# Routed experts behind windowed attention: the first round's chain ahead of the second round's work, the first rows ahead of second-layer weights, and full-height digit matmuls

## The chip, the core and the metric

The kernel runs on one core of a Trainium2 chip. The metric is the device time of one execution in microseconds. Before the change the median of three runs is 535.29 us (534.54 to 538.76). The profiled execution is a fourth one, of 538.62 us; its trace spans 536.9 us, so 1.7 us lie outside the span. TensorE is PE, its weight load PEld, VectorE DVE, ScalarE ACT, GpSimd POOL, and SyncE, which issues most transfers, SP.

## The reference

```python
scores = where(sink or in_window, scale * q @ k.T, -1e9)     # 4 batches, 8 heads, 768 tokens, head_dim 64
x = softmax(scores) @ v                                       # 3072 tokens x 512
logits = x @ w_gate                                           # 8 experts, capacity 384 each
for idx in argsort(-logits.flatten()):                        # greedy: best (token, expert) pair first
    tok, e = idx // E, idx % E
    if assigned[tok] >= 0 or counts[e] >= cap: continue
    assigned[tok] = e; counts[e] += 1
for e in range(E):
    out[assigned == e] = relu(x[assigned == e] @ w1[e]) @ w2[e]   # w1 512x1024, w2 1024x512
```

## The kernel before, in words

**Attention** fills the first 163 us. It writes the tokens to a buffer in HBM and leaves the gate values in `L`.

**Rounds.** The greedy assignment is done in eight rounds (`phase`, k = 0 to 7). Round k finds the one expert that fills up next, and its 384 tokens. It looks for a threshold digit by digit, six digits: DVE compares (`cmp`), 12 or 6 small matmuls count (`cnt`, line 529), DVE turns the counts into eight zeros and ones (`i8`, line 551), one matmul sums them with a constant matrix (`dp`, line 555), DVE takes the maximum (`P`, line 557). Before, `i8` is used to a height of 64 or 32 rows, so that the matmul at line 555 stands on 64 or 32 rows of the array. Then comes the expert's number (`ei`, line 568), a ranking (lines 573 to 598, matmuls at 576, 577 and 602), and the list of tokens (`idx`, lines 606 to 609). Lines 612 to 617 erase the chosen expert and tokens for the next round, and lines 468 to 486 prepare the next round's digits.

**Experts.** Each round feeds one expert. SP reads `ei` and issues eight loads of 512 KB (line 633): chunks 0 to 3 are w1, 4 to 7 are w2. Four buffers `raw` hold them, so chunk 4 may start once chunk 0 has been used. Of each chunk ACT makes a rounded copy `wh` (line 635) and DVE the rest `wl` (line 637). POOL gathers the 384 rows in three indirect transfers `xg` (line 642); PE transposes them (line 650, 12 transposes), and ACT and DVE make `xh` and `xl` (652, 653). The first layer has eight blocks f of four steps, each of three matmuls (line 663); the blocks share two accumulators `ph`, so block f waits until ACT (`hh`, 666) and DVE (`hl`, 667) have emptied block f-2. The second layer has three tiles of eight steps, three matmuls each (675). ACT empties them (678), POOL scatters them (680).

**Order.** Every engine works in order. A list scheduler writes the order of all rounds and experts (`Graph.order`): its priority is the longest remaining path plus a number from the table `BIAS` for the class of the operation (W weights, H hidden, T erasing, and so on, with the round). `warm` (505) puts matmuls without use into PE's gaps until the first expert starts. Rounds and experts overlap: round k+1 is computed while expert k is.

Of the kernel before, what the change touches and what calls it, by code (L numbers as in the profile page):

```python
# [349 lines left out]
CAP=384  # L350
# [62 lines left out]
class Moe:  # L413
# [4 lines left out]
    def __init__(self,ctx,tc,L,idn):  # L418
# [3 lines left out]
        def t(shape,dt,name): return c.tile(shape,dt,name=name)  # L422
# [19 lines left out]
        self.cmp=[t([128,64*NC],BF,f"cmp{j}") for j in range(2)]  # L442
        self.i8=t([128,E+1],BF,"i8"); self.odd=t([64,2*E],F32,"odd"); self.two=t([64,2*E],F32,"two"); self.sw=t([128,3],F32,"sw"); self.P=[t([128,1],F32,f"P{j}") for j in range(2)]
        self.w8=t([128,E],F32,"w8"); self.mx8=t([128,1],F32,"mx8"); self.sel=t([128,E],F32,"sel")
        self.M=t([128,2,NC],BF,"M"); self.xae=t([128,2,NC],F32,"xae"); self.sc=t([128,2*NC],BF,"sc"); self.q=t([128,2,NC],F32,"q"); self.c4=t([128,NC,7],F32,"c4"); self.edge=t([128,6],F32,"edge")
        for j in range(6): g.memset(self.edge[:,j:j+1],64.0*j+63.5)
        self.R=t([128,NC,6],F32,"R"); self.R3=t([128,NC,6],F16,"R3")
        self.ei=[t([1,1],I32,f"ei{j}") for j in range(E)]; self.idx=[t([128,3],I32,f"idx{j}") for j in range(E)]
        self.done=0
    def fill(self,j,n):  # L450
# [56 lines left out]
    def phase(self,g,k):  # L507
        nc=self.nc; V=nc.vector; L=self.L; last=k==E-1; first=k==0; cls=f'R{k}'; slow=2 if first else 1
        u=lambda x: 69+x/.96
        def v(cost,fn,r,w,n=''): return g.add('V',cost,fn,r.split(),w.split(),f'R{k}.{n or w.split()[0]}',cls)  # L510
        def e(cost,fn,r,w,n=''): return g.add('E',cost,fn,r.split(),w.split(),f'R{k}.{n or w.split()[0]}',cls,lat=165)
# [3 lines left out]
        if not last:  # L515
# [6 lines left out]
            for n,(sh,m) in enumerate(STEPS):  # L522
# [27 lines left out]
                v(73,lambda src=src,m=m: V.tensor_scalar(odd[0:m,0:E],src,-1.0,None,op0=OP.mult),tn,'odd')  # L550
                v(73,lambda top=top,m=m: V.scalar_tensor_tensor(self.i8[0:m,0:E],top,float(CAP)-0.5,odd[0:m,0:E],op0=OP.subtract,op1=OP.is_ge),tn+' odd','i8')

                dp,bn=bank()
                wt=self.wt[0] if n==0 else self.wt[1] if n<5 else self.onesb
                e(110,lambda m=m,dp=dp,wt=wt: nc.tensor.matmul(dp[:,0:E],wt[:m],self.i8[:m,0:E],start=True,stop=True),'i8',bn,f'dp{n}')  # L555
                P=self.P[n%2]; Pn=f'P{n%2}'
# [52 lines left out]
        v(75,lambda: V.tensor_tensor(self.idx[k][64:128],r2[64:128,1,:,1],sw[64:128],OP.add),bn+f' swb idxa{k}',f'idx{k}')  # L609
        cls=f'T{k}'  # L610
        if not last:
            v(94,lambda: V.tensor_scalar(self.sel,self.w8,self.mx8,NEG,op0=OP.is_equal,op1=OP.mult),'w8 mx8','sel')
            v(269,lambda: V.tensor_tensor(L,L,self.sel[:,None,:].to_broadcast([128,NC,E]),OP.add),'L sel','L')
            v(138,lambda: V.scalar_tensor_tensor(self.clo,self.w8,self.mx8,self.clo,op0=OP.is_equal,op1=OP.add),'w8 mx8 clo','clo')
            v(u(NC),lambda: V.tensor_tensor(self.m3,c4[:,:,0],c4[:,:,6],OP.subtract),'c40 c4','m3')
# [187 lines left out]
```

## Time and profile before

| | us |
|---|---|
| median of three runs | 535.29 |
| profiled execution | 538.62 |
| its span | 536.9 |
| attention ends, round 0 starts | 163 |
| first matmul of the first expert | 201.85 |
| last matmul of the last expert | 529.8 |

To read it: a timeline row has the start, the duration, the engine, the line, the operation with its output and inputs, and in brackets how long the engine stood idle before and what ended that. Matmuls are pipelined, so their durations overlap; the distance from one start to the next is what a matmul costs. The granted clock is a share of 2.4 GHz; 0.50 is 1.2 GHz.

### The profile page before, as it was taken

The page shows a single profiled execution, that of the slowest core. Times are in us where ns is not written, and L with a number is a line of the kernel's source. Part 1 is how long each engine was busy: PE and PEld are TensorE (multiplying, and loading weights), DVE is VectorE, ACT ScalarE, POOL GpSimd, SP SyncE. Part 2 cuts the span into 40 slices and gives each one's busy share as a digit, 9 for nine tenths or more (in the row PEclk, how much of TensorE's full clock was granted, in tenths as well). Part 3 has the DMA queues.
Part 4 walks back from the last instruction along what each step waited for, and adds up shares of the span by engine and source line. Part 5 has one row for each costly group of instructions (what it writes and reads, how often), then busy time and mean ns, then how long its engine had stood idle before and what let it go on. Part 6 is the DMA issues. An engine that isn't in the chain of part 4 may idle for free.

```text
span 536.9 us, 11136 instructions
## 1 busy us (share of the span) xinstructions
PE 491.7 (92%) x4009; PEld 405.4 (76%) x4009; DVE 351.3 (65%) x1112; ACT 247.8 (46%) x714; POOL 148.6 (28%) x205
## 2 busy tenths in 40 slices
PE   6899999998995589989999999999999999999994
PEld 4687787787883258858877878777788778898983
DVE  2766767767676887965986986887878544541110
ACT  4788887888850043351261451343343334631210
POOL 4667665665440020030040310021310330101001
PEclk7899999999997599998999999999999999999998
DMA  7466665566311280560560641643713644610101
GB/s 238 149 191 175 182 181 169 160 177 169 92 42 40 91 282 2 181 211 2 169 251 13 208 165 59 212 143 108 265 60 123 212 145 153 231 60 20 40 10 50
DMA packets 74935, 72.88 MB, mean 136 GB/s; under 512 B 28032, under 2 KB 57472, under 8 KB 74880
## 3 DMA queue, kind: packets, MB, share of 16 engines
q1 hardware_dynamic: 71040, 59.58, 36.2%
q0 software_dynamic: 3840, 12.59, 6.5%
q8 instruction: 32, 0.52, 0.4%
q14 instruction: 23, 0.19, 0.1%
HBM read 59.57 MB, written 12.58 MB: 134 GB/s over the span
## 4 chain that ended last, share of the span: by engine, by line
PE 60%; DVE 14%; DMA 13%; ACT 7%; issue 3%; SPq 0%; POOLq 0%; POOL 0%; ACTq 0%; DVEq 0%
PE ph L663 19%; PE py L675 15%; DMA raw<-w 10%; PE pp L112 7%; PE pp L74 6%; ACT P L89 4%; DVE wl L637 3%; PE pp L95 3%; PE pp L124 3%; PE pr L529 2%; DMA xg<-x_dram,idx 2%; PE pp L121 2%; ACT wh L635 2%; DVE cmp L459 1%; PE pt L650 1%
## 5 line engine op out<-in xcount | busy, mean ns | idle before, releaser
L635 ACT ACTIVATE wh<-raw 128x1024 fp32r<-128x1024 f32 x64 | 67.6, 1059 | 96.7 <-DMA raw<-w 61.9
L637 DVE TENSOR_TENSOR wl<-raw,wh 128x1024 fp32r<-128x1024 f32 x64 | 78.1, 1221 | 31.4 <-ACT wh L635 30.9
L663 PE MATMUL ph<-xh,wh 128*128 128x384 f32 x256 | 92.7, 362 | 0.0
L663 PE MATMUL ph<-xl,wh 128*128 128x384 f32 x256 | 86.8, 339 | 0.0
L663 PE MATMUL ph<-xh,wl 128*128 128x384 f32 x256 | 86.7, 339 | 0.0
L675 PE MATMUL py<-wh,hh 128*128 128x512 f32 x192 | 78.9, 411 | 1.2 <-ACT yo L678 1.2
L680 POOL DMA_INDIRECT out<-yo,idx x24 | 25.3, 1053 | 196.7 <-ACT yo L678 134.7
L675 PE MATMUL py<-wh,hl 128*128 128x512 f32 x192 | 75.7, 394 | 0.0
L675 PE MATMUL py<-wl,hh 128*128 128x512 f32 x192 | 75.5, 393 | 0.0
L89 ACT ACTIVATE P<-pp,nmx 128x132 f32<-128x132 f32 x192 | 69.1, 369 | 10.1 <-DVE nmx L84 8.4
L666 ACT ACTIVATE hh<-ph 128x384 fp32r<-128x384 f32 x64 | 31.3, 489 | 85.6 <-PE ph L663 68.8
L642 POOL DMA_INDIRECT xg<-x_dram,idx x24 | 28.4, 1182 | 122.9 <-PE pr L555 69.2
L74 PE MATMUL pp<-kk,q 64*128 64x260 f32 (+1 forms) x384 | 58.5, 406 | 2.2 <-ACT P L89 0.8
L667 DVE SCALAR_TENSOR_TENSOR hl<-ph,hh 128x384 fp32r<-128x384 f32 x64 | 35.2, 554 | 38.7 <-ACT hh L666 38.2
L663 PEld LDWEIGHTS ph<-xh,wh 128*128 128x128 f32 x256 | 49.0, 191 | 4.3 <-issue 0.7
L79 DVE COPY_PREDICATED pp<-mprev,pp 128x256 f32<-128x256 int32 x80 | 34.0, 424 | 26.9 <-PE pp L104 16.5
L663 PEld LDWEIGHTS ph<-xl,wh 128*128 128x128 f32 x256 | 48.6, 190 | 2.8 <-DVE xl L653 0.2
L663 PEld LDWEIGHTS ph<-xh,wl 128*128 128x128 f32 x256 | 48.4, 189 | 0.0
L97 POOL TENSOR_SCALAR_AFFINE_SELECT A<-PT 128x512 f32<-128x512 f32 x48 | 31.1, 647 | 49.4 <-ACT PT L96 49.4
L675 PEld LDWEIGHTS py<-wh,hl 128*128 128x128 f32 x192 | 36.0, 188 | 8.7 <-DVE hl L667 0.7
L675 PEld LDWEIGHTS py<-wh,hh 128*128 128x128 f32 x192 | 36.4, 190 | 7.9 <-ACT yo L678 2.0
L84 DVE TENSOR_REDUCE nmx<-pp 128x2 f32<-128x264 f32 x96 | 40.8, 429 | 1.5
(145 smaller groups left out, 843.0 us busy)
## 6 DMA issues: line engine op xcount, KB each, us to landing
raw<-w SPq DMA_DIRECT2D x64, 512.0 KB, 5.0
v<-vd SPq DMA_DIRECT2D x24, 256.0 KB, 3.5
x_dram<-xt SPq DMA_DIRECT2D x24, 256.0 KB, 2.9
kk<-kd SPq DMA_DIRECT2D x23, 264.0 KB, 3.7
q<-qd SPq DMA_DIRECT2D x23, 256.0 KB, 3.8
xg<-x_dram,idx POOLq DMA_INDIRECT x24, 4.9
out<-yo,idx POOLq DMA_INDIRECT x24, 2.8
us<-ud SPq DMA_DIRECT2D x1, 288.0 KB, 4.4
```

What stands on the lines that cost most here:

```text
L74: PE.matmul(sp[:,s,:n],q[p,g,:],kk[p,g,k0:k0+n],start=True,stop=True)
L79: V.copy_predicated(sp[:,:,132:260],mprev[:,None,:].to_broadcast([128,2,128]),sp[:,:,0:128])
L84: V.tensor_reduce(T('nmx',c)[:,2*g:2*g+2],sp[:,:,o:o+132],AX.X,OP.max,negate=True)
L89: A.activation(T('P',c)[:,h,:],sp[:,s,o:o+132],AF.Exp,bias=T('nmx',c)[:,h:h+1],scale=1.0,accum_out=T('sm',c)[:,h:h+1])
L97: def op_A(c,g): G.affine_select(T('A',c)[:,4*g:4*g+4],T('PT',c)[:,4*g:4*g+4],[[0,4],[1,128]],OP.is_ge,0.0,base=0,channel_multiplier=-1)
L112: PE.matmul(av[64*s:64*s+64,hp-2*g,:],T('v',j)[:,h*64:h*64+64],T(x,c)[:,h,:],start=hp==2*g and x=='A',stop=x=='B' or not i,skip_group_chec ...
L635: g.add('A',947,lambda wh=wh,raw=raw: nc.scalar.activation(wh,raw,AF.Copy),[f'raw{n%4}'],[f'wh{s}'],f'H{k}.{j}',f'W{k}')
L637: g.add(e,{'V':1135,'P':2303}[e],lambda wh=wh,wl=wl,raw=raw,e=e: (nc.vector if e=='V' else nc.gpsimd).tensor_tensor(wl,raw,wh.bitcast(F32) ...
L663: nc.tensor.matmul(p[:,0:CAP],x[:,c,:],y[:,c,:],start=c==0 and i==0,stop=c==3 and i==2)
L666: g.add('A',371,lambda f=f,p=p: nc.scalar.activation(self.hh[:,f,:],p[:,0:CAP],AF.Relu),ps,[f'hh{f}'],f'hh{k}.{f}',f'H{k}')
L667: g.add('V',469,lambda f=f,p=p: nc.vector.scalar_tensor_tensor(self.hl[:,f,:],p[:,0:CAP],0.0,self.hh[:,f,:].bitcast(F32),op0=OP.max,op1=OP ...
L675: nc.tensor.matmul(p,x[:,f,ts],w,start=f==0 and i==0,stop=f==7 and i==2)
```

## The change: what it does

Four things. The array `i8` becomes two arrays, zeroed once; the matmul at line 555 uses all 128 rows of one of them. In round 0 the erasing (lines 612, 614, 615) gets a dependency on the token list `idx`. For expert 0 a register load that reads the third gathered tile, and a dependency on it, stand before chunks 4 to 7; nothing uses the register. In the built program the load itself is not there, only its waits: in SP's order the waits for the third gather (and for what was issued before it) stand in the row ahead of the first w2 load of expert 0. The table `BIAS` has other numbers in all entries.

```diff
-        self.i8=t([128,E+1],BF,"i8"); ...
+        self.i8=[t([128,E],BF,f"i8{j}") for j in range(2)]; ...
+        for x in self.i8: g.memset(x,0.0)
...
-                v(73,lambda top=top,m=m: V.scalar_tensor_tensor(self.i8[0:m,0:E],top,float(CAP)-0.5,odd[0:m,0:E],op0=OP.subtract,op1=OP.is_ge),tn+' odd','i8')
+                v(73,lambda top=top,m=m,z=z: V.scalar_tensor_tensor(self.i8[z//4][0:m],top,float(CAP)-0.5,odd[0:m,0:E],op0=OP.subtract,op1=OP.is_ge),tn+' odd',f'i8{z//4}')
...
-                e(110,lambda m=m,dp=dp,wt=wt: nc.tensor.matmul(dp[:,0:E],wt[:m],self.i8[:m,0:E],start=True,stop=True),'i8',bn,f'dp{n}')
+                e(60,lambda z=z,dp=dp,wt=wt: nc.tensor.matmul(dp[:,0:E],wt,self.i8[z//4],start=True,stop=True),f'i8{z//4}',bn,f'dp{n}')
...
-        cls=f'T{k}'
+        cls=f'T{k}'; aft=f' idx{k}' if first else ''
...
-            v(94,lambda: V.tensor_scalar(self.sel,self.w8,self.mx8,NEG,op0=OP.is_equal,op1=OP.mult),'w8 mx8','sel')
+            v(94,lambda: V.tensor_scalar(self.sel,self.w8,self.mx8,NEG,op0=OP.is_equal,op1=OP.mult),'w8 mx8'+aft,'sel')
...
+            if k==0 and j==4:
+
+                g.add('S',100,lambda: nc.sync.value_load(self.xg[2][0:1,0:1].bitcast(I32)),['xg2'],['rowed'],'rowed','L0')
...
-            g.add('D',1460,ld,[f'reg{k}'],[f'raw{n%4}'],f'L{k}.{j}',f'L{k}')
+            g.add('D',1460,ld,[f'reg{k}']+(['rowed'] if k==0 and j>3 else []),[f'raw{n%4}'],f'L{k}.{j}',f'L{k}')
...
-            self.weights(g,k); self.rows(g,k); self.mlp(g,k)
+            if k==0: self.rows(g,k); self.weights(g,k); self.mlp(g,k)
+            else: self.weights(g,k); self.rows(g,k); self.mlp(g,k)
...
-BIAS={'G0': -792535, 'G1': -546488, ...
+BIAS={'G0': 295629, 'G1': 162254, ...
```

The order of the attention part is the same on every engine. Behind it the new table moves work on all of them. Line numbers of the change are one higher than before from line 449 on, and four higher from line 633 on.

**DVE, the end of round 0.** `sw` and `idx` are the token list, `di`, `xb`, `cmp<-xb` are round 1's digits, `wl` is expert 0's first weights. Before:

```order
416 L475 TENSOR_TENSOR s<-vm,f 128x24
417 L477 TENSOR_SCALAR di<-s 128x24
418 L478 TENSOR_SCALAR di<-s 128x24
419 L482 TENSOR_SCALAR di<-s 128x24
420 L606 TENSOR_SCALAR sw<-pr_2411 64x3
421 L607 TENSOR_SCALAR sw<-pr_2411 64x3
422 L479 CAST xb_103<-di 128x24
423 L608 TENSOR_TENSOR idx_142<-pr_2411,sw 64x3
424 L483 TENSOR_SCALAR di<-s 128x24
425 L459 TENSOR_TENSOR cmp_109<-xb_103,grid 128x1536
426 L609 TENSOR_TENSOR idx_142<-pr_2411,sw 64x3
```

With the change:

```order
402 L599 TENSOR_TENSOR R_134<-R,tid 128x144
403 L607 TENSOR_SCALAR sw<-pr_2414 64x3
404 L608 TENSOR_SCALAR sw<-pr_2414 64x3
405 L609 TENSOR_TENSOR idx_143<-pr_2414,sw 64x3
406 L610 TENSOR_TENSOR idx_143<-pr_2414,sw 64x3
407 L613 TENSOR_SCALAR sel<-w_118,mx_119 128x8
408 L616 TENSOR_TENSOR m_98<-c_125 128x24
409 L615 SCALAR_TENSOR_TENSOR clo<-w_118,mx_119,clo 128x8
410 L614 TENSOR_TENSOR L<-L,sel 128x192
411 L617 TENSOR_TENSOR fin<-fin,m_98 128x24
412 L641 TENSOR_TENSOR wl_2383<-raw_2367,wh_2371 128x1024
```

Twenty rows of the erasing and of round 1 have moved behind the token list; round 1's digits now stand between and behind the first three `wl`.

**ACT, the start of expert 0.** `wh` are the weight chunks in their order, `xh` the rows, `hh` the first layer's blocks. Before:

```order
230 L635 ACTIVATE wh_2371<-raw_2367 128x1024
231 L635 ACTIVATE wh_2372<-raw_2364 128x1024
232 L635 ACTIVATE wh_2373<-raw_2365 128x1024
233 L635 ACTIVATE wh_2374<-raw_2366 128x1024
234 L652 ACTIVATE xh_2395<-pt_2404 128x384
```

With the change:

```order
230 L639 ACTIVATE wh_2374<-raw_2370 128x1024
231 L656 ACTIVATE xh_2398<-pt_2407 128x384
232 L656 ACTIVATE xh_2398<-pt_2408 128x384
233 L656 ACTIVATE xh_2398<-py_2411 128x384
234 L656 ACTIVATE xh_2398<-py_2412 128x384
235 L639 ACTIVATE wh_2375<-raw_2367 128x1024
236 L639 ACTIVATE wh_2376<-raw_2368 128x1024
237 L639 ACTIVATE wh_2377<-raw_2369 128x1024
238 L670 ACTIVATE hh_2402<-ph_2409 128x384
239 L639 ACTIVATE wh_2378<-raw_2370 128x1024
```

The rows now come ahead of w2's chunks, and three of those chunks (4, 5, 6) stand between the rows and the first block's `hh`.

**DVE, round 1's token list.** `wl` are the chunks 0, 1, 2 of expert 1. Before:

```order
532 L607 TENSOR_SCALAR sw<-pr_2411 64x3
533 L637 TENSOR_TENSOR wl_2388<-raw_2364,wh_2376 128x1024
534 L667 SCALAR_TENSOR_TENSOR hl_2400<-ph_2406,hh_2399 128x384
535 L550 TENSOR_SCALAR odd<-pr_2410 64x8
536 L608 TENSOR_TENSOR idx_143<-pr_2411,sw 64x3
537 L637 TENSOR_TENSOR wl_2389<-raw_2365,wh_2377 128x1024
538 L551 SCALAR_TENSOR_TENSOR i_111<-pr_2410,odd 64x8
539 L609 TENSOR_TENSOR idx_143<-pr_2411,sw 64x3
540 L637 TENSOR_TENSOR wl_2390<-raw_2366,wh_2378 128x1024
```

With the change:

```order
519 L607 TENSOR_SCALAR sw<-pr_2414 64x3
520 L608 TENSOR_SCALAR sw<-pr_2414 64x3
521 L617 TENSOR_TENSOR fin<-fin,m_98 128x24
522 L609 TENSOR_TENSOR idx_144<-pr_2414,sw 64x3
523 L618 TENSOR_SCALAR pen<-fin 128x24
524 L610 TENSOR_TENSOR idx_144<-pr_2414,sw 64x3
525 L641 TENSOR_TENSOR wl_2391<-raw_2367,wh_2379 128x1024
```

The list no longer stands behind two of expert 1's `wl`. On PE all 24 second-layer steps of expert 0 now stand ahead of expert 1's first block; before, five of them (3.45 us at three matmuls of 0.23 us each) stood behind it.

## Rows read from the trace of the kernel before

**Rows 1.** Stretches: borders, length; busy us (instructions) of PE, PEld, DVE, ACT, POOL; clock, DMA share, GB/s.

```profile
194.00:198.00 4.00, 3.31 (x29) 2.31 (x29) 2.88 (x7) 1.30 (x2) 0.00 (x0) 1.00 0.99 343
...
201.80:247.00 45.20, 41.55 (x245) 34.62 (x242) 35.17 (x115) 16.07 (x24) 4.22 (x4) 0.96 0.36 117
247.00:450.00 203.00, 195.72 (x1184) 162.44 (x1184) 152.84 (x515) 73.68 (x114) 35.96 (x31) 1.00 0.44 147
450.00:530.00 80.00, 80.00 (x395) 71.19 (x393) 23.34 (x31) 23.75 (x37) 8.75 (x9) 1.00 0.22 76
```

**Rows 2.** Timeline of PE, a digit matmul (line 555) inside the first layer.

```profile
207.95 0.34 PE L663 MATMUL ph<-xh,wl 128*128 128x384 f32 x1
208.22 0.17 PE L555 MATMUL pr<-i,wt 32*128 32x8 bf16 x1
208.60 0.34 PE L663 MATMUL ph<-xl,wh 128*128 128x384 f32 x1
```

**Rows 3.** Timeline of PE, two full-height small matmuls (576, 577) inside the first layer.

```profile
216.82 0.33 PE L663 MATMUL ph<-xh,wh 128*128 128x384 f32 x1
...
217.17 0.34 PE L663 MATMUL ph<-xh,wl 128*128 128x384 f32 x1
217.34 0.20 PE L576 MATMUL pr<-M,ltf 128*128 128x48 bf16 x1
...
217.68 0.34 PE L663 MATMUL ph<-xl,wh 128*128 128x384 f32 x1
```

**Rows 4.** Line 555 from 200 to 450 us, digits one to five.

```profile
L555 PE MATMUL pr<-i,wt x28: 161/174/177, 203.8 to 404.5; 32*128 32x8 bf16 x18, 64*128 64x8 bf16 x10
```

**Rows 5.** Timeline of DVE, the end of round 0 and the first `wl`.

```profile
186.65 0.16 DVE L606 TENSOR_SCALAR sw<-pr 64x3 f32<-64x3 f32 x1
...
187.27 0.94 DVE L459 TENSOR_TENSOR cmp<-xb,grid 128x1536 bf16<-128x1536 bf16 x1
...
188.24 0.16 DVE L609 TENSOR_TENSOR idx<-pr,sw 64x3 int32<-64x3 f32 x1
...
188.60 1.22 DVE L637 TENSOR_TENSOR wl<-raw,wh 128x1024 fp32r<-128x1024 f32 x1
```

**Rows 6.** Timeline of POOL, round 0's third gather.

```profile
192.49 1.29 POOL L642 DMA_INDIRECT xg<-x_dram,idx  x1 [0.30 <-issue]
```

**Rows 7.** The tile `xg` from 185 to 240 us, six gathers.

```profile
DMA to landing us min/median/max: 4.6/6.1/7.0
```

**Rows 8.** Timeline of PE: round 0's selection, the last rows' transposes, the first expert's first matmul.

```profile
184.80 0.82 PE L602 MATMUL pr<-R,cmp 128*128 128x12 f16 x12 [2.02 <-DVE R L598]
...
200.53 0.42 PE L650 MATMUL pt<-idt,xg 128*128 128x128 f32 x2
...
201.85 0.47 PE L663 MATMUL ph<-xh,wh 128*128 128x384 f32 x1
```

**Rows 9.** Timeline of ACT, expert 0's third chunk.

```profile
190.66 1.06 ACT L635 ACTIVATE wh<-raw 128x1024 fp32r<-128x1024 f32 x1 [1.83 <-DMA raw<-w]
```

**Rows 10.** The tile `raw` at 218.4 us, expert 1's first chunk.

```profile
DMA to landing us min/median/max: 3.5/3.5/3.5
```

**Rows 11.** Timeline of DVE, round 1's expert number.

```profile
217.47 0.13 DVE L568 TENSOR_SCALAR ei<-mx 1x1 int32<-1x1 f32 x1
```

**Rows 12.** Timeline of PE, from expert 0 to expert 1.

```profile
240.35 0.40 PE L675 MATMUL py<-wl,hh 128*128 128x512 f32 x1
240.58 0.39 PE L675 MATMUL py<-wh,hl 128*128 128x512 f32 x1
242.92 0.64 PE L650 MATMUL pt<-idt,xg 128*128 128x128 f32 x3 [1.95 <-DVE xl L653]
...
244.17 0.67 PE L663 MATMUL ph<-xh,wh 128*128 128x384 f32 x1
```

**Rows 13.** Stretches of 1 us there, first and last of four (columns as in Rows 1).

```profile
243.00:244.00 1.00, 1.00 (x11) 0.97 (x12) 0.49 (x2) 0.40 (x1) 0.00 (x0) 0.62 0.00 0
...
246.00:247.00 1.00, 1.00 (x5) 0.80 (x3) 0.00 (x0) 0.00 (x0) 0.00 (x0) 0.67 0.00 0
```

More of the change, by code (lines that the diff above doesn't have):

```diff
@@ L442, in __init__ @@
         self.cmp=[t([128,64*NC],BF,f"cmp{j}") for j in range(2)]
-        self.i8=t([128,E+1],BF,"i8"); self.odd=t([64,2*E],F32,"odd"); self.two=t([64,2*E],F32,"two"); self.sw=t([128,3],F32,"sw"); self.P=[t([128,1],F32,f"P{j}") for j in range(2)]
+        self.i8=[t([128,E],BF,f"i8{j}") for j in range(2)]; self.odd=t([64,2*E],F32,"odd"); self.two=t([64,2*E],F32,"two"); self.sw=t([128,3],F32,"sw"); self.P=[t([128,1],F32,f"P{j}") for j in range(2)]
         self.w8=t([128,E],F32,"w8"); self.mx8=t([128,1],F32,"mx8"); self.sel=t([128,E],F32,"sel")
@@ L609, in phase @@
         v(75,lambda: V.tensor_tensor(self.idx[k][64:128],r2[64:128,1,:,1],sw[64:128],OP.add),bn+f' swb idxa{k}',f'idx{k}')
-        cls=f'T{k}'
+        cls=f'T{k}'; aft=f' idx{k}' if first else ''
         if not last:
-            v(94,lambda: V.tensor_scalar(self.sel,self.w8,self.mx8,NEG,op0=OP.is_equal,op1=OP.mult),'w8 mx8','sel')
+            v(94,lambda: V.tensor_scalar(self.sel,self.w8,self.mx8,NEG,op0=OP.is_equal,op1=OP.mult),'w8 mx8'+aft,'sel')
             v(269,lambda: V.tensor_tensor(L,L,self.sel[:,None,:].to_broadcast([128,NC,E]),OP.add),'L sel','L')
-            v(138,lambda: V.scalar_tensor_tensor(self.clo,self.w8,self.mx8,self.clo,op0=OP.is_equal,op1=OP.add),'w8 mx8 clo','clo')
-            v(u(NC),lambda: V.tensor_tensor(self.m3,c4[:,:,0],c4[:,:,6],OP.subtract),'c40 c4','m3')
+            v(138,lambda: V.scalar_tensor_tensor(self.clo,self.w8,self.mx8,self.clo,op0=OP.is_equal,op1=OP.add),'w8 mx8 clo'+aft,'clo')
+            v(u(NC),lambda: V.tensor_tensor(self.m3,c4[:,:,0],c4[:,:,6],OP.subtract),'c40 c4'+aft,'m3')
             v(94,lambda: V.tensor_tensor(self.fin,self.fin,self.m3,OP.add),'m3 fin','fin')
@@ L708 @@
 WIN=[57, 20025, 0]
-BIAS={'G0': -792535, 'G1': -546488, 'G2': -633612, 'G3': 704367, 'G4': -575163, 'G5': 500108, 'G6': 10533, 'G7': -133134, 'H0': 299567, 'H1': 1372456, 'H2': 338684, 'H3': -266186, 'H4': -364686, 'H5': 2369818, 'H6': -896421, 'H7': -76664, 'L0': -840419, 'L1': 654324, 'L2': 12318, 'L3': 841779, 'L4': -170296, 'L5': -628514, 'L6': 692631, 'L7': 213847, 'M0': -22297, 'M1': -7980, 'M2': -8511, 'M3': -8278, 'M4': -9159, 'M5': -4063, 'M6': -12918, 'M7': -21024, 'R0': 704402, 'R1': -18122, 'R2': -4203, 'R3': 234584, 'R4': 179907, 'R5': 1909682, 'R6': 384962, 'R7': 883127, 'T0': -19659, 'T1': 1773027, 'T2': 1669104, 'T3': -859854, 'T4': 14341, 'T5': 12376, 'T6': -896985, 'W0': -36172, 'W1': -549668, 'W2': -381652, 'W3': -368567, 'W4': 365326, 'W5': -359470, 'W6': -526682, 'W7': -1545768, 'X0': -33219, 'X1': 579241, 'X2': 526590, 'X3': 309896, 'X4': 231846, 'X5': 2813021, 'X6': 9673, 'X7': 602071, 'Y0': 317574, 'Y1': 172957, 'Y2': 613051, 'Y3': 949410, 'Y4': -77758, 'Y5': -1031147, 'Y6': -573493, 'Y7': -678043}
+BIAS={'G0': 295629, 'G1': 162254, 'G2': -279312, 'G3': 1563873, 'G4': 1916835, 'G5': 932476, 'G6': 733051, 'G7': -243162, 'H0': -37865, 'H1': 19849, 'H2': 91381, 'H3': 988353, 'H4': 747095, 'H5': 376035, 'H6': -482536, 'H7': 1000667, 'L0': 868944, 'L1': 361431, 'L2': -470007, 'L3': -1363030, 'L4': 41186, 'L5': 77034, 'L6': 79739, 'L7': -945789, 'M0': -1013394, 'M1': -1229497, 'M2': -103038, 'M3': 69487, 'M4': 187558, 'M5': 618607, 'M6': -184857, 'M7': -185071, 'R0': 20465, 'R1': 1980837, 'R2': 72703, 'R3': 62626, 'R4': 606374, 'R5': 360221, 'R6': 645534, 'R7': -18418, 'T0': 265289, 'T1': -260247, 'T2': 771717, 'T3': -353978, 'T4': 507303, 'T5': 923769, 'T6': 1091256, 'W0': -324369, 'W1': -204177, 'W2': 520839, 'W3': 15091, 'W4': 717057, 'W5': 73461, 'W6': 506221, 'W7': 639832, 'X0': 584716, 'X1': 216444, 'X2': 327140, 'X3': 730156, 'X4': 747134, 'X5': 763428, 'X6': 1245410, 'X7': 235969, 'Y0': 1049838, 'Y1': -1062891, 'Y2': -751289, 'Y3': -323402, 'Y4': -991979, 'Y5': -1207049, 'Y6': -429487, 'Y7': -379383}
 def attention_general(ctx,tc,qd,kd,vd,iwd,ident,idn,x_dram,L,n_sink,window):
```

## The prediction

> **What bounds the kernel now.** I read the stretches first. From the first expert's first matmul to the last expert's end, PE is busy nearly throughout: it idles 3.65 us of 45.2 around the first expert, 7.28 us of 203 in the middle, and nothing from 450 on [rows 1]. So behind 201.85 us time can be won in three ways: PE starts earlier, PE gets fewer or cheaper small matmuls, or one of the 11 us of idle goes. Then I read PE's timeline for the price of a small matmul [rows 2 to 4], DVE's and POOL's for what the first matmul waits for [rows 5 to 8], and the passage from expert 0 to expert 1, the largest hole [rows 11 to 13]. All sums are differences against the profiled execution (538.62 us, of which 1.7 lie outside the span); that execution is 3.3 us above the median of the runs, and I take the difference off the median, 535.29.
>
> **Part 1, the digit matmuls on all rows.** A first-layer matmul costs 0.175 us (216.82 to 217.17 is two of them) [rows 3]. Around a digit matmul, 207.95 to 208.60 holds two first-layer matmuls and it: 0.65 - 0.35 = 0.30 us [rows 2]. Two other small matmuls in a row, on all 128 rows, cost 217.17 to 217.68 less 0.35 = 0.16 us together [rows 3]. So a digit matmul on all rows should cost at most 0.16, a saving of 0.14 or more; if one of the two at 217.34 is worth a quarter of that, 0.18. There are 34 behind 200 us: 28 of the first five digits [rows 4] and one of the last digit in each of six rounds. 34 x 0.14 to 0.18 is 4.8 to 6.1 us where PE is the bound; a few stand in holes, where they save nothing. I take 5.0. Ends: 0 (the price is that of any change of kind on PE) and 6.1. DVE still writes only 64 or 32 rows, and the two clearings of the arrays are on POOL, in the start of the attention, not on the path.
> What the row shows is that the matmul's own 0.17 us is no longer than its neighbours'; the cost lies before and after it. The Trainium skill, TensorEngine Tiling (Array Packing), Key Properties, says that changing the tiling mode drains TensorE; by that rule the saving is there at every one of the 34, some 5 us. The Trainium skill, TensorE: Matmul & The Clock Gate, Why this matters for your kernels, says that a single matmul of 32 rows takes the time of one of 128; by that the height buys nothing and the 5 us fall away. The trace agrees with both as far as it goes, and the second is a rival below.
>
> **Part 2, the first matmul earlier.** Before, the selection matmuls end at 184.80 + 0.82 = 185.62 [rows 8], but DVE reaches `sw` at 186.65 and the last `idx` at 188.24, behind round 1's digits and a compare of 0.94 [rows 5]. With the twenty rows moved behind it, `sw` can start at 185.7 and four dependent steps of 0.2 end at 186.5; some 0.6 of the rows moved stood ahead of the selection too (an estimate from their 0.2 to 0.35 each), so 185.9. That is 2.5 us earlier. The third gather was issued 4.25 us after `idx` began [rows 5, 6] and a gather takes 4.6 to 7.0 us to land [rows 7]; so it lands at 194.6 to 197.0, and the last transposes and the first matmul follow within 1.3 (200.53 to 201.85 [rows 8]): 195.9 to 198.3.
> DVE sets a later limit. Behind `idx` it has now 1 us of erasing, three `wl` of 1.22 [rows 5], of which the third must wait for ACT's `wh` (190.66 + 1.06 = 191.7 before [rows 9]), then round 1's digits, some 1.5 us, its compare 0.94, the fourth `wl` 1.22, the digit rows 0.5 and the first `xl` 0.55: 191.9 + 1.22 + 1.5 + 0.94 + 0.3 + 1.22 + 0.5 + 0.55 = 198.1. PE's order has round 1's first count and digit matmul ahead of the first block, so it cannot pass. I take 198.3, a gain of 3.5. Ends: 6 (the gathers' earliest) and 1 (the third chunk comes a few us later because the gathers now run beside it).
>
> **Part 3, what is late next: w2.** Chunks 4 to 7 now wait on SP for the third gather. I take landing at 195.5; the loads then have the transfer engines to themselves, the first lands 3.5 us later [rows 10] and each further one 1.55 (512 KB at the 343 GB/s of 194 to 198 [rows 1]). The third is there at 202.1, its `wh` at 203.2 (1.06 [rows 9]), and only then ACT reaches block 0's `hh`, DVE its `hl`: 204.4. Blocks 0 and 1 are 24 matmuls of 0.175, done at 198.3 + 4.2 + 0.5 = 203.0. Block 2 waits some 1.5 us, and block 4 another 1 behind DVE's `wl` of chunk 7. Before, nothing of this kind stood there. I take a loss of 2.5. Ends: 0 (all landed in time) and 5. The clock may also be at 1.2 GHz at the first block, since PE has little to do from 192 to 198; while block 2 waits anyway this costs nothing, otherwise up to 1.5.
>
> **Part 4, from expert 0 to expert 1.** Before, PE stood from 240.58 to 242.92, started expert 1 at 244.17 [rows 12], lost 0.38 + 0.50 + 0.50 + 0.33 = 1.7 us to a clock of 0.50 in the four us from 243 on [rows 13], and idled 3.65 us in all there [rows 1]. Five second-layer steps, 5 x 3 x 0.23 (240.35 to 240.58 [rows 12]) = 3.45 us, were still to do. Round 1's list had stood behind two `wl` that waited for loads. With the change the list comes first, and expert 0 is finished before expert 1. But round 1's expert number also comes later: 217.47 before [rows 11]; now it follows more first-layer steps on PE and four late `wl` on DVE, by count of the steps some 222, so expert 1's loads come 4.5 us later. Adding its chunks at 1.55, the conversions of 1.06 and 1.22 behind each, and the three gathers behind the list, expert 1's first block starts at about 243 (an estimate of mine; the third w2 chunk's `wl` stands on DVE ahead of the first `xl` and sets it), with 3.45 us less left over and at full clock: 1.2 + 3.45 + 1.7 = 6.3 us ahead of before. Of these 1 is Part 1's and 3.5 - 2.5 is Parts 2 and 3's, so this part gives 4. Ends: 0 and 5.4 (the idle and the clock wholly gone).
>
> **Part 5, rounds 2 to 7.** The table moves hundreds of rows on every engine. The middle idles 7.28 us and the end nothing [rows 1]. In the new order I followed each expert's list to its gathers and transposes with the durations above: the lists of rounds 2 and 5 stand behind one to four `wl`, which costs 2 to 3 us each; the others meet their place within 1. I take a gain of 2 for the whole. Ends: 7 (all idle gone) and a loss of 5.
>
> **Sum.** -5.0 - 3.5 + 2.5 - 4.0 - 2.0 = -12.0 us: 526.6 for an execution like the profiled one, **523.3** for the median. 1% of the time, 5.4 us, is about what a measurement of this kernel can tell from no change: the border is at 529.9.
>
> **Rivals.**
> The digit matmul keeps its price. For it: its own duration is that of its neighbours, and the 0.30 could be the price of a single small matmul of another type. Against it: the two at 217.34 changed type as well and cost half. Then 528.3.
> The new order loses in the middle what it wins at the start: Part 5 at its bad end, +5 in place of -2, gives 530.3. For it: PE idles only 7.28 us in 203 there, so there is little left to win and many places to lose. Against it: these idles are of one kind, rows or digits that come late, and the new order has fewer `wl` ahead of them.
> Slower: the wait for the third gather starves round 1. If that gather lands at 199.4 as before (192.49 + 6.9 [rows 6, 7]), chunk 4 is issued at 200, 10 us after its place before; round 1's digits, which stand behind its `wl` on DVE, and with them expert 1's number come at 227, and expert 1 starts at 254 in place of 244.17; less 3.45 and 1.7 that is 5 us late, and with the middle at +5, Part 1 at its lower third and no gain in Part 2 some 7 us over: 542. It decides where the third gather lands behind 199. Against it: the list leaves DVE 2.5 us earlier, and the held loads are the very traffic that slowed that gather.
> Better: the middle's 7.28 us all go and block 2 does not wait: 523.3 - 5.3 - 2.5 = 515.5.
>
> **Chances.** Forecast 0.55, its own range 518 to 528.5; price of the digit kept 0.12; lost in the middle 0.20; slower 0.07; better 0.06. Faster by over 1%: 0.54 + 0.09 + 0.08 + 0.06 = 0.77; slower by over 1%: 0.07; the rest, 0.16, within 1%. The range goes from the better case to a little over the case lost in the middle: 514 to 533; it leaves out the slower case and the far ends.
>
> **What would show it.** Part 1: 0.16 us or less around a digit matmul. Part 2: the list's last row at about 186, the third gather landed by 197, the first block at 198.3. Part 3: ACT's third w2 chunk ahead of the first `hh`, and block 2 waiting for `hl` with PE idle 1 to 2 us. Part 4: expert 1's first block at 243 or earlier, at a clock of 1.00, with no second-layer step of expert 0 behind it. Part 5: PE idle under 7 us from there to 450. I am wrong if w2's wait shows as more than 5 us of idle in the first expert, or if transposes wait for gathers at more than two of the later experts.

## The result and the profile after

| | before | after |
|---|---|---|
| median of 20 runs each | 535.74 us (532.3 to 538.76) | 531.19 us (527.34 to 536.25) |
| ratio after/before | | 0.9918, 95% interval 0.9894 to 0.9942 |
| span of the first profiled execution | 536.9 us (time 538.62) | 530.6 us (time 532.35) |
| spans of further profiles | 533.3, 532.9 us | 528.3, 531.1, 527.1 us |

The change makes the kernel faster by 0.8%, 4.4 of 535.29 us. Forecast were 12.0; the measured time lies near the upper end of the range.

The stretches of the first profile after, with the borders and columns of [rows 1]:

```profile
194.00:198.00 4.00, 3.75 (x32) 3.21 (x30) 3.97 (x12) 2.28 (x5) 0.00 (x0) 1.00 0.70 257
...
201.80:247.00 45.20, 41.47 (x249) 34.72 (x249) 34.59 (x114) 17.51 (x26) 7.66 (x6) 0.96 0.37 130
247.00:450.00 203.00, 194.58 (x1171) 164.25 (x1170) 154.11 (x511) 76.72 (x115) 34.35 (x28) 0.98 0.45 151
450.00:530.00 80.00, 73.91 (x385) 66.10 (x383) 22.00 (x39) 20.76 (x35) 10.70 (x11) 0.98 0.19 63
```

PE idles 8.42 us of 203 in the middle, more than the 7.28 of before, and the clock there is 0.98 in place of 1.00. The last row ends with the work, 6 us earlier.

PE's timeline around a digit matmul, the counterpart of [rows 2]:

```profile
212.73 0.34 PE L667 MATMUL ph<-xh,wl 128*128 128x384 f32 x1
212.90 0.18 PE L556 MATMUL pr<-i,wt 128*128 128x8 bf16 x1
212.94 0.42 PE L667 MATMUL ph<-xh,wh 128*128 128x384 f32 x1
213.20 0.34 PE L667 MATMUL ph<-xl,wh 128*128 128x384 f32 x1
```

212.73 to 213.20 holds two first-layer matmuls and the digit's: 0.47 - 0.35 = 0.12 us, where 0.30 stood. The same stretch of before holds one more first-layer matmul than the three rows of [rows 2]:

```profile
208.32 0.44 PE L663 MATMUL ph<-xh,wh 128*128 128x384 f32 x1
```

The place is no exception. Where a digit matmul stands among full matmuls at full clock and nothing waits (25 or 26 places in each profile), the median price is 0.31 us in three profiles before and 0.13 in four after. The line's own duration did not fall; its group from 195 to 450 us, counterpart of [rows 4]:

```profile
L556 PE MATMUL pr<-i,wt x30: 166/180/187, 195.6 to 412.2; 128*128 128x8 bf16 x30
```

The list, DVE's timeline (its first and last row), counterpart of [rows 5]:

```profile
184.18 0.16 DVE L607 TENSOR_SCALAR sw<-pr 64x3 f32<-64x3 f32 x1 [0.91 <-PE pr L603]
...
184.74 0.16 DVE L610 TENSOR_TENSOR idx<-pr,sw 64x3 int32<-64x3 f32 x1
```

The tile `xg` from 183 to 240 us, counterpart of [rows 7]:

```profile
DMA to landing us min/median/max: 4.2/5.5/6.4
```

PE's timeline, the first expert's first block, block 2, and expert 1's first block, counterparts of [rows 8, 12]:

```profile
195.78 0.47 PE L667 MATMUL ph<-xh,wh 128*128 128x384 f32 x1
...
204.05 0.44 PE L667 MATMUL ph<-xh,wh 128*128 128x384 f32 x1 [2.59 <-DVE hl L671]
...
242.12 0.67 PE L667 MATMUL ph<-xh,wh 128*128 128x384 f32 x1
```

ACT's timeline ahead of that 2.59 us wait; the third w2 chunk, then the first `hh` (compare [rows 9]):

```profile
201.97 1.06 ACT L639 ACTIVATE wh<-raw 128x1024 fp32r<-128x1024 f32 x1 [2.21 <-DMA raw<-w]
202.94 0.47 ACT L670 ACTIVATE hh<-ph 128x384 fp32r<-128x384 f32 x1
```

The list ends at 184.90, not 188.40; the first block starts at 195.78, not 201.85; block 2 then waits 2.59 us behind the held chunk. This much is as forecast, if larger. Stretches of 1 us of the same execution (columns as in [rows 1]) show three places at half clock (1.2 GHz) further on, one in each row:

```profile
241.00:242.00 1.00, 1.00 (x4) 0.66 (x4) 0.97 (x3) 0.48 (x2) 0.00 (x0) 0.50 0.00 0
...
279.00:280.00 1.00, 1.00 (x4) 0.81 (x3) 1.00 (x2) 0.71 (x2) 0.85 (x1) 0.50 0.70 250
360.00:361.00 1.00, 1.00 (x4) 0.78 (x3) 1.00 (x3) 0.00 (x0) 0.00 (x0) 0.50 0.00 0
```

### The profile page after: what moved, and what is told of

Read it like the earlier page. It is cut to its first block, busy times and chain, and to the rows that moved or that the text cites. A ratio compares the mean times of both kernels' runs of the same rounds, so it can differ in the third digit from the quotient of the medians.

```text
span 530.6 us, 11127 instructions
## 1 busy us (share of the span) xinstructions
PE 487.3 (92%) x3999; PEld 404.7 (76%) x3999; DVE 350.1 (66%) x1112; ACT 248.7 (47%) x714; POOL 152.0 (29%) x207
## 5 line engine op out<-in xcount | busy, mean ns | idle before, releaser
L684 POOL DMA_INDIRECT out<-yo,idx x24 | 28.5, 1189 | 176.9 <-ACT yo L682 117.3
```

The costliest lines, as they stand in the source:

```text
L684: st=nc.gpsimd.indirect_dma_start(out=self.out,out_offset=bass.IndirectOffsetOnAxis(ap=idx[:,t:t+1],axis=0),in_=y,in_offset=None)
```

## The experiments

Each kernel's ratio is to the kernel before, timed beside it, with its 95% interval. Theories were made in this order: first the parts of the change by themselves, then the clock, then the one execution, then the waits in the later rounds. Two edits were never run by themselves: the dependency of the erasing on `idx`, and the rows ahead of the weights in round 0.

In the lists of places below, `R3.dp0` is the digit matmul of round 3's first digit, `R2.cnt1` the counting of round 2's second digit, and `X1.0.2` a transpose of expert 1's third gathered tile.

**Digits alone.** In before's program and order, only the digit matmul's height:

```diff
-nc.tensor.matmul(dp[:,0:E],wt[:m],self.i8[:m,0:E],...)
+nc.tensor.matmul(dp[:,0:E],wt,self.i8[z//4],...)
```

> The kernel before, word for word in its order, with the digit matmuls on all 128 rows and nothing else. Theory A (TensorE's stream is the bound in the experts, so what a small matmul costs there is paid): 34 digit matmuls lose 0.17 us each, so 5 to 6 us less, 530 where before is 535.7, ratio 0.990. Rival B (the rounds on VectorE and the weight loads set the pace in the middle, so TensorE's savings turn into waits): the traced cost of each digit matmul falls all the same, but the time falls by less than 2 us, ratio above 0.996. Rival C (the height has no price): the excursion stays at 0.30 us and the time at 535.7.

531.77 us, 0.9957 [0.9938, 0.9976]: 2.3 us, about half of Part 1. That is nearer rival B: the price of a digit matmul falls to a median of 0.13 us here too, but less than half of it arrives. From the first expert's first matmul to PE's last one PE idles 12.7 us in this run's profile, where it idled 10.9, 9.7 and 7.8 in three profiles of before: in this execution part of what was saved is waited.

**The change without the digits.** The new program and order, the digit matmul on 64 or 32 rows again:

```diff
-matmul(dp[:,0:E],wt,self.i8[z//4],...)
+matmul(dp[:,0:E],wt[:m],self.i8[z//4][:m],...)
```

> The changed kernel, same order, with the digit matmuls back on 64 or 32 rows. Theory A: 5 to 6 us more than the changed kernel, 536.5 to 537, about as slow as before or slower. Rival B: under 2 us more, 532 to 533.

534.24 us, 0.9998 [0.9967, 1.0028]: nearer theory A. So the new order alone gives nothing that can be measured, where Parts 2 to 5 together said 7.0 us. By the difference to 0.9918 the digits are worth 4.3 us here, give or take 2.1.

**No hold.** The w2 loads no longer wait for the third gather, in an unchanged order of instructions:

```diff
-lambda: nc.sync.value_load(self.xg[2][0:1,0:1].bitcast(I32))
+None
```

> The changed kernel, same order, without the wait of the w2 loads for the third gather. Theory A (the hold moves a wait, from the rows to block 2): the gathers run beside the loads again, the third lands 2 to 3 us later (196 instead of 193.3), the first block starts 2 to 3 us later, and the wait of block 2 for the hidden part (2.6 us) goes; the sum within 1.5 us of the changed kernel's 531.2. Rival D (the hold is the gain of the lead-in): 533.5 or more.

529.82 us, 0.9921 [0.9893, 0.9949]: the changed kernel's time within 2 us, theory A. The wait moved. PE's waits from 195 to 244 us in its profile (line, releaser; us in total, times, longest):

```profile
PE pt L654 <- DMA xg<-x_dram,idx: 1.8, 2, 1.2
PE pr L530 <- DVE cmp L460: 0.8, 1, 0.8
PE ph L667 <- DVE hl L671: 0.3, 1, 0.3
```

Block 2's wait for `hl` is 0.3 us. The transposes wait 1.8 for the gathers, of which 1.25 are expert 0's at 194.70 and the rest expert 1's; another 0.70 of expert 0's lie just ahead of the window. The third gather landed 6.2 us after its issue, at 196.0, where with the hold it took 4.2 and landed at 193.3. Their rows of the tile `xg`, with the hold and without:

```profile
DMA to landing us min/median/max: 4.2/4.2/4.2
DMA to landing us min/median/max: 6.2/6.2/6.2
```

**Old table.** All edits, the old table's numbers:

```diff
-BIAS={'G0': 295629, ...}
+BIAS={'G0': -792535, ...}
```

> All edits of the changed kernel with the old table of priorities. The traces of before and after say that from the start of expert 1 on the new order gave back what the digits saved (5 us). Theory A: with the old table that is not given back, 526 to 529. Rival E (any order gives it back, because the middle is bound elsewhere): 530 to 533.

532.73 us, 0.9987 [0.996, 1.0014]. Theory A fell, the time is rival E's: without the new table there is less gain, not more. The old numbers do not bring back the old order here: on the changed dependencies they write a third one, so this run does not compare the two orders.

**The same two kernels again**, unaltered, since the first profiles held half-clock stretches at different places.

> The changed kernel once more, nothing altered, for a second profile. Theory A (the granted clock falls to 1.2 GHz behind some of the holes in TensorE's work, and which of them is chance): the waits over 0.3 us stand at the same instructions as in the first profile of it, within about 0.5 us each (R2.cnt1, R3.dp0, R5.cnt1 among them), but the stretches at half clock inside the experts do not: none to three of them, at other places, and the span moves by 1.7 us for each one gained or lost (528 to 533). Rival B (the falls belong to the order): the same three stretches, behind the same three waits, and the span within 1 us of 530.6.

> The kernel before once more, nothing altered, for a second profile. Theory A (the first profile, whose own time was 538.62 us against a median of 534 to 536, held a hole and a fall of the clock at 240 to 247 us that most executions do not hold): span 531.5 to 534.5 us, the wait of 2.1 us at 240.6 and the half-clock stretch behind it smaller or gone, so that part of the gain I took from the start of expert 1 was a gain over that one execution. Rival B (the execution was a fair one): span 536 to 538, the same hole and fall at 240 to 247 us.

Spans 528.3 and 533.3 us, with no half clock from 195 us to the end of the work in either: theory A in both. Only its price was too high: three half-clock stretches at 1.7 us each were gone, and the span fell by 2.3. The passage to expert 1 in before_again, PE's timeline, beside [rows 12]:

```profile
240.64 0.55 PE L650 MATMUL pt<-idt,xg 128*128 128x128 f32 x3 [0.49 <-DVE xl L653]
...
241.57 0.42 PE L663 MATMUL ph<-xh,wh 128*128 128x384 f32 x1
```

And its clock there, beside [rows 13]:

```profile
243.00:244.00 1.00, 1.00 (x7) 0.73 (x6) 0.65 (x6) 0.00 (x0) 0.00 (x0) 1.00 0.00 0
```

The wait for `xl` is 0.49 us in place of 1.95, the clock is 1.00, and expert 1 starts 2.6 us earlier than in [rows 12] without any change.

**Holes filled.** 39 useless matmuls, as in the first round's warming, ahead of eleven waiting instructions of the changed kernel:

```diff
+if t[4] in FILL: self.warm(self.pr[0],FILL[t[4]])
 t[2]()
+FILL={'X1.0.2':3,'R2.cnt1':4,'R3.dp0':8,'R4.dp0':2,...,'X6.0.0':6,'X6.0.2':3}
```

> The changed kernel with 39 useless 384-column matmuls (0.16 us each, 6.3 us in all) set on TensorE's queue directly ahead of eleven instructions that waited 0.4 to 2.0 us in its profile, a little less filling than each wait. They compute nothing that is used. Theory A (falls of the clock behind the holes cost 1.7 us each, up to 5.1 us in an execution): the granted clock stays at 2.4 GHz from 195 us to the end of the work, the waits are filled and no longer holes, and the median goes down by 1 to 4 us, ratio to before 0.985 to 0.990. Rival B (what eats the gain is the waits themselves, the falls are rare or cost little in the median): clock held, but the time stays within 0.3% of the changed kernel's (ratio 0.990 to 0.994). Rival C (the filling delays the work behind it): 533 to 537.

529.07 us, 0.9902 [0.987, 0.9934], clock 1.00 from 201.8 to 450 us: between A and B. PE's waits from 244 to 450 us:

```profile
PE pr L506 <- DVE i L552: 3.0, 3, 1.5
PE pr L556 <- DVE i L552: 1.3, 1, 1.3
PE pr L530 <- DVE cmp L460: 0.5, 1, 0.5
```

At digit places the filling (L506) itself waited, 3.0 us in all, and then only added work. Filling cannot give back a wait: what PE waits for comes no sooner. It can only keep the clock up.

**Work pulled ahead.** In place of filling, up to 13 steps of the matrix products are moved ahead of the same eleven instructions, each time the next step on PE's queue, if its inputs are issued before:

```diff
+PULL={'X1.0.2':1,'R2.cnt1':1,'R3.dp0':2,...,'X6.0.0':2,'X6.0.2':1}
+ev.insert(p,ev.pop(q))
```

> The changed kernel, but one step (two at R3.dp0 and X6.0.0) of the matrix products moved ahead of each of the same eleven waiting instructions on TensorE's queue; 13 moves, nothing added or removed. Theory A (TensorE is the bound, and what the change saved on it is lost as some 9 us of waits at these places, because the rounds' chain on VectorE and the gathers did not become shorter with it): the waits are filled with work that is needed anyway, 4 to 8 us less, ratio 0.978 to 0.985, fewer falls of the clock. Rival B (the rounds' chain with its gathers is the bound of these stretches): each of the eleven comes later by what was put ahead of it, the waits turn up at later instructions of the same chain or at the next expert's start, and the time stays within 0.3% of the changed kernel's. Rival C: worse by 2 us and more, since a step of 0.7 us delays a chain that waited 0.4.

530.06 us, 0.9919 [0.9893, 0.9946]: rival B in its time. PE's waits from 244 to 450 us fell to 6.9 us in its profile (7.8 to 9.4 in four of the changed kernel), yet the time did not move.

**New start, old rest.** The new table's numbers for rounds and experts 0 and 1, the old ones for 2 to 7:

```diff
+BIAS={c:(new if int(c[1])<2 else old)[c] for c in new}
```

> All edits of the change, with the new table's numbers for rounds and experts 0 and 1 and the old table's for 2 to 7. Theory A (the new order wins some 5 us up to expert 1's start and its own steps in rounds 2 to 7 then cost about 2 us of what the full-height digit matmuls save there): expert 1 starts where it does in the changed kernel (231 to 234 us for its first transposes), and from there to the end it is 1.5 to 3 us shorter, 528 to 529.5, ratio 0.986 to 0.989. Rival B (the later stretches wait for the rounds' chain and the gathers in either order): within 0.3% of the changed kernel (0.990 to 0.994). Rival C (the old numbers do not fit a start that is 5 us earlier): 533 and more.

534.77 us, 0.9981 [0.9945, 1.0017]: not A; nearest C. What one table wins at the start does not survive the other's rest.

**What 4.9 us of TensorE are worth**, in both kernels:

```diff
-for i,(x,y) in enumerate(...):
+for i,(x,y) in [z for z in enumerate(...) if not (k>0 and z[0]==1 and c==2 and f%2==0)]:
```

> The kernel before with 28 first-layer matmuls left out (the second of three products at one of the four row blocks, in every other column block of experts 1 to 7): 28 x 0.174 = 4.9 us less on TensorE, every other engine's instructions and the order the same. It measures what 4.9 us of TensorE time are worth in this order from expert 1 on. Theory A (TensorE's time comes through less than whole, since the chain of the rounds on VectorE does not shorten with it and TensorE waits longer for it): 2 to 3.5 us less, ratio 0.9935 to 0.9965. Rival B (TensorE is the bound, each us arrives): 4.5 to 5 us less, ratio 0.991 or below.

> The changed kernel with the same 28 first-layer matmuls left out, 4.9 us less on TensorE. Theory A (in the new order the later experts already wait for the rounds' chain at more places, so still less of it arrives): 0.5 to 2.5 us below the changed kernel, ratio to before 0.987 to 0.991. Rival B (TensorE is the bound): 4.5 to 5 us below it, ratio 0.982 to 0.984.

Before: 531.77 us, 0.9956 [0.9927, 0.9985], 2.4 us of 4.9: theory A. After: 526.86 us, 0.9825 [0.9773, 0.9877], 5.0 us below 0.9918 with an uncertainty of 3.1: nearer B, against my expectation. In the new order TensorE's time seems to arrive more fully, as with the digits (4.3 against 2.3 us); neither pair of intervals is narrow enough to call it shown.

**No hold and pulled work.** Meant as the best version, with the moves of the run before, two more at R4.dp1, and filling at five places:

```diff
-g.add('D',1460,ld,[f'reg{k}']+(['rowed'] if k==0 and j>3 else []),...)
+g.add('D',1460,ld,[f'reg{k}'],...)
```

> The order of the changed kernel, second-layer weights not held, 15 steps of the matrix products moved ahead of twelve instructions that waited on TensorE, and 16 useless 384-column matmuls at five further waits that the run with moved steps showed. Theory A (waits of TensorE still cost, and filling both kinds takes 2 to 4 us out): 527 to 529.5, ratio 0.985 to 0.990, span 524 to 526, no half clock from 195 us on. Rival B (the rounds' chain sets these stretches): 529.5 to 531.5, ratio 0.990 to 0.994, as each of its parts alone.

537.96 us, 1.0066 [1.0038, 1.0094]. It tells nothing on the theories: here the dependency left the planner's graph too, and the planner wrote another order, so that the moves fell at places that no profile had asked for. It does show that another order, with 2.6 us of useless matmuls in it, can cost 1.5% against the changed kernel.

**Third profiles, and Part 4 by itself.** The last kernel is before with eleven useless matmuls ahead of three instructions at the passage:

```diff
+FILL={'R2.cnt1':5,'R2.dp1':2,'X1.2.0':4}
```

> The kernel before, nothing altered, a third profile. Theory A (the 2.1 us wait at X1.2.0 and the half-clock stretch behind it, 3.7 us together, are in few executions): the wait there is under 1.2 us, the clock at 2.4 GHz from 195 us on or half at another place, expert 1's first matmul at 238 to 241 us, span 532 to 534.5. Rival B (they are in most): both there again, expert 1's first matmul at 242 to 243.5, span 535.5 to 537.5.

> The changed kernel, nothing altered, a third profile. Theory A (which waits are followed by half clock is chance): none to two half-clock stretches inside the experts, not the three places of the first profile, waits over 0.3 us between 262 and 371 us of 6 to 8 us in all (in before 4.6 and 5.3), span 527.5 to 530. Rival B: the three stretches at 240, 278 and 360 us again, span 530 to 531.

> The kernel before, its order unchanged, with 11 useless 384-column matmuls (0.16 us each, 1.8 us) ahead of three instructions of round 2 and expert 1's rows that waited there: five ahead of R2.cnt1, two ahead of R2.dp1, four ahead of X1.2.0. No wait over 0.5 us is left between 230 and 243 us and the clock stays at 2.4 GHz there. Theory A (the long wait with its half clock is in few executions): the median stays within 1 us of before, ratio 0.998 to 1.002. Rival B (it is in most, so that Part 4's 4.0 us were there to win): 2 to 3.5 us less, ratio 0.9935 to 0.996.

before_third: span 532.9 us, the wait 0.59 us, expert 1 from 243.81, clock 1.00 there, half at 202 to 205 instead: A, but for a start of expert 1 nearer B's. after_third: span 531.1 (my range ended at 530), half clock at 204 and at 241, none at 278 or 360, and waits of 5.4 us in all from 262 to 371, under the 6 to 8 expected: theory A, but for its numbers. e12: 534.62 us, 0.9999 [0.9971, 1.0026]: theory A. PE's waits from 195 to 244 us in its profile:

```profile
PE pr L529 <- DVE cmp L459: 0.9, 1, 0.9
PE pt L650 <- DMA xg<-x_dram,idx: 0.6, 2, 0.4
PE ph L663 <- DVE xl L653: 0.3, 1, 0.3
PE pr L555 <- DVE i L551: 0.3, 1, 0.3
```

The 1.9 us for `xl` ahead of the transposes is gone, the clock is at 2.4 GHz there, and the median stays. Since filling gives back no wait, this shows that the fall of the clock at this place cost the median little. That the wait itself is mostly short is shown by the profiles: at this place of the same order it is 1.95, 0.49 and 0.59 us in three of before, 0.93 in the run with only the digits changed and 0.26 in the one with 28 matmuls left out; the clock fell behind the first alone.

**The best version.** No hold (in an unchanged order) with the 39 useless matmuls; then with 24 of them, without the digit places (the line below is what leaves the list); the last beside the changed kernel on the same chip:

```diff
-'R3.dp0':8,'R4.dp0':2,'R5.dp0':1,'R6.dp1':4
```

> The changed kernel's order with the second-layer weights not held and the 39 useless matmuls of the earlier filled run ahead of the same eleven waits: the two versions that came out at or a little under the changed kernel, together. Theory A (holes and the half clock behind some of them cost 1 to 2 us in the median): 527.5 to 529.5, ratio to before 0.986 to 0.9905. Rival B (they cost nothing in the median): 530 to 531.5, ratio 0.991 to 0.994.

> The changed kernel, nothing altered, timed beside the next one, with a fourth profile. Ratio to before 0.990 to 0.994, as first measured. Waits of TensorE from 244 to 450 us 8 to 9.5 us in all (in three profiles of before 5.5 to 7.7), if the order sets them and not the execution.

> The changed kernel's order, second-layer weights not held, 24 useless matmuls ahead of seven waiting instructions; the four digit places of the earlier filled runs are left out, since there the useless matmuls waited themselves (3.0 us of waiting stood at them in that profile) and only added to the time. Theory A (a hole that is filled is worth something, by the clock behind it): 527.5 to 529.5 us, ratio at least 0.003 under the changed kernel's of this job. Rival B (the waits and falls are exchanged for others and cost nothing in the median): ratio within 0.003 of it.

529.55 us, 0.9884 [0.9846, 0.9923]; changed kernel 530.91 us, 0.9924 [0.9896, 0.9952], its waits from 244 to 450 us 7.8, just under the 8 expected; 529.36 us, 0.9888 [0.9861, 0.9915]. All beat before, and both filled kernels lie where theory A has them. Against the changed kernel timed beside it the last is 0.36% lower, 1.9 us, with overlapping intervals: likely better, not shown.

## Why the prediction was wrong

The direction and the first steps hold; the sum was 7.6 us too large. Two terms of the order carry it, **Part 4** and **Part 5**.

**Part 1** holds in price and nearly in sum: 0.12 us around a digit matmul (at most 0.16 forecast; median 0.13), 4.3 us, give or take 2.1, by the difference of the runs with and without it, 5.0 forecast. In before's order only 2.3 arrive. The rival that the price is kept is refuted. The Trainium skill, TensorE: Matmul & The Clock Gate, Why this matters for your kernels, says that a single matmul of 32 rows takes the time of one of 128. The rows agree for the matmul's own duration (174 ns in [rows 4], 180 ns now) and show that the price lies in its neighbours, 0.30 against 0.12 us around it. That agrees with what TensorEngine Tiling (Array Packing), Key Properties, of the Trainium skill says of draining when the mode changes.

**Part 2** was too small: first block 195.78, 196.60, 196.11 and 198.01 us in four profiles after, 201.85, 201.54 and 202.34 in three before, 5.3 us on average against 3.5. The list ended 1 us before my estimate. DVE did set the first block, through round 1's first digit, as the text says, but 2.3 us sooner than its sum (198.1). Rows of DVE and PE in the first profile after: the third `wl`, the first digit's `i`, the digit matmul that waits for it.

```profile
190.43 1.23 DVE L641 TENSOR_TENSOR wl<-raw,wh 128x1024 fp32r<-128x1024 f32 x1
...
195.35 0.16 DVE L552 SCALAR_TENSOR_TENSOR i<-pr,odd 64x8 bf16<-64x8 f32 x1
...
195.57 0.17 PE L556 MATMUL pr<-i,wt 128*128 128x8 bf16 x1 [0.25 <-DVE i L552]
```

The third `wl` began at 190.43, where the sum had 191.9, and the first matmul did not stand behind the first `xl`, which came after `i`.

**Part 3** holds as described: the third w2 chunk ahead of the first `hh`, block 2 waiting for `hl` 2.6, 1.2, 2.0 and 0.9 us, 1.7 on average against a term of 2.5. As a cost of the hold it is not shown: without the hold the transposes wait instead, expert 1's first block stands at 240.7 in place of 241.8 to 243.5, and the time is the same within 2 us.

**Part 4** is the first step that failed. Its 4.0 us were read from [rows 12, 13] as if every execution held them. Of three profiles of the unchanged kernel one does; the wait is 1.95, 0.49 and 0.59 us, the clock at 243 us 0.62, 1.00 and 1.00. Spans without it are 533.3 and 532.9 in place of 536.9 us, and keeping the clock up there leaves the median where it was (0.9999). Of the signs, expert 1's first block came at 242.12, before 243, and all of expert 0's second layer ahead of it, but at a clock of 0.50, not 1.00. The profiled execution lay 3.3 us above the median. I took the difference off the median, as if all its losses were in the median too; those 3.3 us were largely the very hole that Part 4 was to win: a wait 1.4 us longer than in the two other profiles, and 1.7 us of half clock.

**Part 5** is the second: -2.0 forecast, about +2 by the waits measured. The text named its sign of failure, PE idle over 7 us from there to 450. PE's waits from 244 to 450 us, in before_again:

```profile
PE pt L650 <- DMA xg<-x_dram,idx: 3.4, 5, 1.4
PE pr L555 <- DVE i L551: 1.5, 2, 1.0
PE py L675 <- ACT hh L666: 1.2, 1, 1.2
PE pr L529 <- DVE cmp L459: 0.7, 1, 0.7
PE pt L650 <- DVE xl L653: 0.4, 1, 0.4
PE py L675 <- ACT yo L678: 0.3, 1, 0.3
PE py L675 <- DVE hl L667: 0.2, 1, 0.2
```

And in after_again:

```profile
PE pt L654 <- DMA xg<-x_dram,idx: 3.5, 3, 2.1
PE pr L556 <- DVE i L552: 3.3, 4, 1.3
PE pr L530 <- DVE cmp L460: 1.6, 3, 1.0
PE ph L667 <- DVE hl L671: 0.3, 1, 0.3
PE py L679 <- ACT yo L682: 0.2, 1, 0.2
```

In sum 7.7 against 8.9 us. Over all profiles: 6.8, 7.7 and 5.5 before, 8.2, 8.9, 9.4 and 7.8 after. The waits for gathers are about the same (2.7 against 2.9 us on average); those for the digits (`i`) and compares (`cmp`) of the rounds' chain on DVE are 2.6, 2.2 and 2.0 us before, 4.8, 4.9, 4.8 and 5.3 after. It is the order that makes them, by one profile each of the two mixed kernels. Their rows for `i` and `cmp`, the new order with short digits, then the old order with tall ones:

```profile
PE pr L556 <- DVE i L552: 5.6, 5, 2.4
PE pr L530 <- DVE cmp L460: 0.9, 2, 0.6
...
PE pr L556 <- DVE i L552: 2.2, 3, 0.9
PE pr L530 <- DVE cmp L460: 0.9, 2, 0.7
```

That is 6.5 against 3.1 us, in waits of 8.8 and 7.7 in all. I had followed the lists to their gathers and transposes, and never the six digits of a round to the place at which PE takes them.

**The ledger**, in means of three profiles before and four after. The first block starts 5.3 us earlier, and block 2 waits 1.7. Expert 1's first block stands at 243.2 us before (244.17, 241.57, 243.81) with 3.45 us of expert 0's second layer left to do, and at 242.3 after (242.12, 241.82, 243.46, 241.96) with none: 4.3 us ahead. That is 5.3 - 1.7 and 0.7 more, no more than the 1 us of Part 1 that the forecast has there, so nothing is left for Part 4. Against the first profile alone the lead is 5.5 us, where the forecast had 1.2 + 3.45: the steps moved as forecast, and the base was one slow passage.

From expert 1's first block to PE's last matmul PE idles 7.0 us before and 8.9 after, and half clock costs it 0.4 and 1.2. The remaining work is 3.5 us shorter, and this is the digits': in the new order with short digits the work is as long as before (273.6 us). Rows of that stretch (columns as in [rows 1]) in before_again and after_again:

```profile
241.57:526.56 284.99, 277.10 (x1588) 235.32 (x1586) 177.59 (x551) 98.15 (x152) 43.82 (x40) 1.00 0.38 126
241.82:521.59 279.77, 270.69 (x1583) 232.00 (x1581) 179.72 (x560) 98.28 (x151) 47.65 (x39) 1.00 0.39 127
```

So 4.3 + 3.5 - 1.9 - 0.8 = 5.1 us, as far as the mean spans differ; by the ratio of the times it is 4.4. The order's own share is -0.1 +/- 1.6 us by the runs with short digits and -2.1 +/- 1.6 by those with tall ones (0.9918 against 0.9957), where Parts 2 to 5 said -7.0. That Part 4's 4.0 us were not there is shown; that the later waits cost the time what they measure is argued: with steps moved ahead of them the waits fell to 6.9 us and the time stayed.

The rival "lost in the middle", given 0.20 with 530.3 us, is closest in time and in kind. That its time is so close is in part luck: it has Part 4's 4.0 us, which did not come, and a loss of 5 in the middle, where about 2 were lost. The slower rival did not come: the third gather landed by 193.3 us in the first profile after, far from 199. What was said against it, that the held loads are the traffic that slowed that gather, is what the run without the hold shows (196.0). The half-clock stretches were my first theory of the missing gain. They differ from execution to execution: three, none, two, and one at 194 us in four profiles after. The executions with none or only the early one took 531.02 and 529.57 us, with spans of 528.3 and 527.1; those with three and two took 532.35 and 532.82. What the clock costs in the median is known only by the filled kernels, which came out at most 1.9 us lower, and that is not shown either. What the waits themselves cost no run measures.

## What to carry to other kernels

Before a hole in one profiled execution is counted as a gain, look whether a second execution of the same kernel holds it. An execution that lies above its median can hold losses that the median lacks, and a difference against it should not be taken off the median. Where steps are moved, follow every chain to the place where the bound engine takes its result, the small ones of each round too, not only those that the change was about. A small matmul of another height among full-height ones was paid for around it (0.31 against 0.13 us), not in its own duration (174 against 180 ns): price it by the starts of its neighbours. Useless matmuls in a wait can keep the clock up; they cannot give the wait back.

## What the runs showed of the hardware

The granted clock fell to 1.2 GHz behind waits of 0.6 and 0.8 us in the first profile after (241 to 244 us at 0.50), and not behind the 2.6 us wait at 201 us of the same execution; in the third profile it fell at that very place, around a wait of 2.0 us. At the first digit of round 3 it fell behind a wait of 1.9 us in the first profile, and not behind 1.3 and 1.8 us in the second and fourth. So a single wait does not say whether the clock falls.

Loads that were held back made the third gather land sooner: 4.2, 3.7 and 5.2 us after its issue in three profiles after, 6.2 and 6.4 in two kernels of the same order without the hold, 6.9 and 8.0 in two profiles before. Expert 1's gathers, where nothing was held, took 5.2 to 7.0 in the same profiles before and after. The 2 us did not reach the time. The first block stood behind DVE's first digit as well: it started 2.5 us behind the landing with the hold (195.78), and 1.0 behind it without (196.99).
